# The last eight odd tiles of a dilated convolution: transposes and projections over two overlapping blocks of 128 columns, so that all TensorE operations there have one shape

## The chip, the cores and the metric

The kernel runs on one core of one Trainium2 chip. Times are device microseconds of one execution. Every run quoted here was of the state "fast"; nothing is concluded from a slow one. TensorE (PE, its weight loads PEld), VectorE (DVE), ScalarE (ACT), GpSimd (POOL) and SyncE (SP) are the engines; "SPq" lines of a profile are instructions on SyncE's own sequencer, here issues of DMA stores.

## The reference, cut to what matters

```python
B, T, D, K = (2, 16000, 144, 15)           # x: B,T,D   w: K,D,2D   w_o: D,D   all bf16
h = sum over i of xp[:, pad - 2*i : pad - 2*i + T, :] @ w[i]      # 15 taps, dilation 2
z = tanh(h[..., :D]) * sigmoid(h[..., D:])
return z @ w_o
```

The point that matters is D = 144 = 128 + 16: for the last product each tile of z must be turned round, and 144 channels do not fit in the 128 rows or columns of the array.

## The kernel before: the parts that the change and the argument touch

Each of the 128 partitions owns 250 successive positions. A *tile* is one position for all partitions: 128 x 144 values of z in the SBUF tensor `Z`. Eight tiles make an octet, kept side by side in a slot of `Z` (8 x 144 = 9 x 128 columns). All octets but the last two are turned round by a DMA transpose of nine whole blocks of 128 columns and projected with `WOR`, which holds `w_o` at every row offset that such a block can need, with zeros elsewhere.

The last two octets are handled differently so that the end of the kernel does not wait for that DMA. Their even tiles still take it; their odd tiles (dl = 1, 7, 3, 5, in two octets: eight tiles, four pairs) are transposed on TensorE, evicted from PSUM, projected, evicted again and stored pair by pair. This is that part:

```python
def ship_pair(o0, o1, dl):
    zs = (zslot(o0, dl), zslot(o1, dl))          # the two octets' slots
    pa, pb = _Bank(), _Bank()                    # two PSUM banks
    ...
    for i in range(2):
        fns.append(transpose(PSb[:, bank pa, 128*i : ...],    Z[:, zs[i], dl*D : dl*D + 128]))      # 128*128
        fns.append(transpose(PSb[0:16, bank pb, 128*i : ...], Z[:, zs[i], dl*D + 128 : dl*D + D]))  # 128*16
    g.add("dve", ... tensor_copy(zt(q, 0, 256), bank pa) ...)               # Xr<-PS on VectorE
    g.add("act", ... activation(zt(q, 256, 256)[0:16], bank pb, Copy) ...)  # Xr<-PS on ScalarE
    for i in range(2):
        fns.append(matmul(PS[:, ...], lhsT=zt(q, 128*i, 128),                rhs=WOR[:, 0, :]))     # 128*128
        fns.append(matmul(PS[:, ...], lhsT=zt(q, 256 + 128*i, 128)[0:16, :], rhs=WOR[0:16, 1, :]))  # 16*128
    g.add("act", ... activation(OS, PS, Copy) ...)                          # OS<-PS on ScalarE
...
for dl in dls[:2]:  ship_pair(o0, o1, dl)
for dl in dls[:2]:  store_both(o0, o1, dl)       # one store of 72 KB for the pair
for o in (o0, o1):
    project_some(o, (0, 2, 4, 6)); store_some(o, 0)
for dl in dls[2:]:  ship_pair(o0, o1, dl); store_both(o0, o1, dl)
...
def _(e):                                        # SyncE's program
    emit("sp", e)                                # all loads, DMA transposes and stores, in order
    for s, v in g.finals: e.wait_ge(s, v)        # then every DMA semaphore once
```

A list scheduler in the kernel puts the operations of each engine in order from estimated durations. (Here and in the diffs below access patterns are shortened.)

## Time and profile before

The median is 333.14 us (332.87 to 333.17 in three runs); the profiled run spans 331.2 us.

| What | before |
|---|---|
| PE busy, share of the span | 98% |
| first of these transposes starts | 320.05 us |
| first product of the last gate unit (line 727) starts | 322.06 us |
| end of ScalarE's last eviction | 328.11 us |
| SyncE begins to issue the last store | 328.61 us |
| span ends | 331.2 us |

From the page of before, section 1 (busy time, share of the span, instructions):

```profile
PE 323.0 (98%) x2736; PEld 249.4 (75%) x2736; DVE 302.6 (91%) x662; ACT 259.4 (78%) x626; POOL 17.2 (5%) x30
```

TensorE bounds the kernel, but a busy PE says nothing of how fast its instructions follow one another. For that, take the chain of waits of before in the tail: start, length of the step, engine, destination and line. L772 and L773 are the transposes of 128 and of 16 columns, L863 an ordinary projection, L780 and L782 the pair's projections over 128 and over 16 rows.

```profile
320.21 0.06 PE PS L772
320.27 0.15 PE PS L773
320.42 0.16 PE PS L772
320.58 0.15 PE PS L773
320.74 0.61 PE PS L863 x8
...
323.57 0.06 PE PS L780
323.64 0.16 PE PS L782
323.80 0.17 PE PS L780
...
327.48 0.20 PE PS L782
327.67 0.02 issue
327.70 0.41 ACT OS L786
```

An operation that follows one of the same shape takes a step of 0.06 us; after every change of shape the step is 0.15 to 0.17 us. The weight loads show where the time goes: here the first load of 16 columns begins 0.15 us after the start of the transpose ahead of it (320.20 against 320.05 us). The timeline of before (start, length, engine, line, operation) shows what this does to the rest. The last gate unit's input from VectorE was ready at 320.25 + 0.77 = 321.02 us, yet its first product starts at 322.06, behind two pairs of transposes and the ordinary projections between them (a gate unit is here the group of products that one tanh and one sigmoid read):

```profile
320.25 0.77 DVE L1024 TENSOR_TENSOR PS<-PS,Xp 128x576 f32<-128x576 f32 x1
322.06 0.41 PE L727 MATMUL PS<-WA,GD 128*128 128x288 bf16 x2
324.61 1.42 SPq L808 DMA_DIRECT2D out_dram<-OS  x2
327.04 0.35 SPq L851 DMA_DIRECT2D out_dram<-OS  x1
327.43 0.42 SPq L799 DMA_DIRECT2D out_dram<-OS  x1
327.70 0.41 ACT L786 ACTIVATE OS<-PS 128x288 bf16<-128x288 f32 x1 [0.28 <-PE PS L782]
327.90 1.32 SPq L808 DMA_DIRECT2D out_dram<-OS  x2
```

The last lines are the end: ScalarE evicts the last pair (the bracket says that it idled 0.28 us for TensorE), and SyncE issues the remaining stores. The last line is two issues of 0.61 us each; the second begins at 328.61 us.

### The profile page before, as it was taken

What the parts mean: (1) busy time and instruction counts of PE and PEld (TensorE: products, weight loads), DVE (VectorE), ACT (ScalarE), POOL (GpSimd) and SP (SyncE); (2) the same over time, 40 slices, a digit from 0 to 9 for tenths busy, and PEclk for the clock granted to TensorE, in tenths of its full rate; (3) what the DMA queues carried; (4) which work ended last, traced back from release to release, by engine and by line L of the source; (5) the groups of instructions that cost most, each with busy time, mean ns of one, the idle gap of its engine ahead of it and who ended that gap; (6) DMA issues with size and microseconds to landing.
All of it is one profiled execution on the core that took longest, in us unless ns stands there. A gap on an engine that the chain in (4) does not pass through costs nothing.

```text
span 331.2 us, 7123 instructions
## 1 busy us (share of the span) xinstructions
PE 323.0 (98%) x2736; PEld 249.4 (75%) x2736; DVE 302.6 (91%) x662; ACT 259.4 (78%) x626; POOL 17.2 (5%) x30
## 2 busy tenths in 40 slices
PE   7899999999999999999999999999999999999995
PEld 7787867777777777777777777777777777777773
DVE  1999889999999999999999999999999999895682
ACT  3327577979798897979798897979889797787754
POOL 8740000000000000000000000000000000000000
PEclk9999999999999999999999999999999999999997
DMA  8889942928759392956839394874919194411443
GB/s 213 265 124 210 218 121 43 191 84 169 174 99 206 81 207 100 182 158 126 218 63 194 117 177 135 146 200 93 248 38 200 38 154 117 97 48 38 107 109 107
DMA packets 112509, 46.46 MB, mean 140 GB/s; under 512 B 103822, under 2 KB 106303, under 8 KB 112477
## 3 DMA queue, kind: packets, MB, share of 16 engines
q1 hardware_dynamic: 111961, 45.68, 64.6%
q8 instruction: 21, 0.34, 0.4%
q0 software_dynamic: 512, 0.33, 0.4%
q14 instruction: 11, 0.09, 0.1%
q10 hardware_dynamic: 4, 0.01, 0.0%
HBM read 11.82 MB, written 9.22 MB: 64 GB/s over the span
## 4 chain that ended last, share of the span: by engine, by line
PE 93%; DVE 5%; ACT 1%; issue 1%; POOL 0%; POOLq 0%
PE PS L727 81%; PE PS L832 8%; DVE Xp L1012 2%; PE PS L541 1%; DVE WC L616 1%; DVE V L673 1%; DVE PS L1033 0%; PE PS L782 0%; PE PS L863 0%; PE PS L780 0%; PE PS L773 0%; DVE XA L574 0%; PE PS L772 0%; DVE PS L1024 0%; DVE Z L756 0%
## 5 line engine op out<-in xcount | busy, mean ns | idle before, releaser
L1012 DVE TENSOR_TENSOR Xp<-PS,UX 128x576 f32<-128x576 f32 x90 | 65.2, 752 | 7.0 <-PE PS L727 6.4
L1024 DVE TENSOR_TENSOR PS<-PS,Xp 128x576 f32<-128x576 f32 x90 | 68.2, 758 | 3.6 <-ACT UX L960 1.8
L727 PE MATMUL PS<-WA,GD 128*128 128x288 bf16 x360 | 69.8, 286 | 0.3 <-DVE PS L1024 0.3
L748 ACT ACTIVATE TS<-PS 128x288 f16<-128x288 f32 x125 | 51.4, 411 | 14.7 <-PE PS L727 10.0
L891 ACT ACTIVATE PS<-PS 128x288 f32<-128x288 f32 x120 | 45.4, 401 | 17.5 <-PE PS L727 17.5
L751 ACT ACTIVATE TS<-PS 128x288 f16<-128x288 f32 x125 | 50.7, 405 | 0.0
L960 ACT ACTIVATE UX<-PS 128x576 f32<-128x576 f32 x60 | 39.0, 651 | 14.7 <-PE PS L727 13.4
L727 PE MATMUL PS<-WS,GU 128*128 128x288 bf16 x210 | 44.1, 286 | 0.0
L655 ACT ACTIVATE STB<-XBc 128x512 bf16<-128x512 bf16 x60 | 35.9, 630 | 10.0 <-DVE V L673 5.6
L840 ACT ACTIVATE OS<-PS 128x432 bf16<-128x432 f32 (+1 forms) x88 | 42.4, 488 | 0.5
L832 PE MATMUL PS<-WOR,ZT 128*128 128x144 bf16 (+1 forms) x322 | 42.3, 253 | 0.0
L727 PEld LDWEIGHTS PS<-WA,GD 128*128 128x128 bf16 x360 | 34.2, 98 | 10.4 <-DVE PS L1024 0.8
L756 DVE TENSOR_TENSOR Z<-TS 128x288 bf16<-128x288 f16 x125 | 37.3, 300 | 4.0 <-ACT TS L751 3.8
L727 PE MATMUL PS<-WB,XB 128*128 128x288 bf16 x140 | 37.6, 286 | 0.0
L727 PE MATMUL PS<-WB,BF 128*128 128x288 bf16 x120 | 34.3, 286 | 0.0
L727 PE MATMUL PS<-WB,BE 128*128 128x288 bf16 x120 | 34.3, 286 | 0.0
L832 PEld LDWEIGHTS PS<-WOR,ZT 128*128 128x128 bf16 x322 | 28.0, 98 | 6.1 <-ACT OS L840 0.6
L727 PE MATMUL PS<-WD,DD 128*128 128x288 bf16 x180 | 31.9, 286 | 0.2 <-ACT PS L891 0.2
L727 PE MATMUL PS<-WA,DD 128*128 128x288 bf16 x180 | 30.9, 287 | 0.3
L727 PE MATMUL PS<-WC,V 128*128 128x288 bf16 x180 | 30.6, 286 | 0.0
L727 PE MATMUL PS<-WT,DU 128*128 128x288 bf16 x120 | 24.8, 288 | 0.7 <-DVE Xp L1012 0.7
L727 PEld LDWEIGHTS PS<-WS,GU 128*128 128x128 bf16 x210 | 20.2, 98 | 5.7 <-ACT PS L891 0.3
(89 smaller groups left out, 521.2 us busy)
## 6 DMA issues: line engine op xcount, KB each, us to landing
Xr<-in_x_dram SPq DMA_DIRECT2D x15, 576.0 KB, 4.0
out_dram<-OS SPq DMA_DIRECT2D x29, 288.0 KB, 2.8
WA<-in_w_dram SPq DMA_DIRECT2D x3, 288.0 KB, 5.0
ZT<-Z SPq DMA_TRANSPOSE x32, 3.4
Xp<-in_x_dram SPq DMA_DIRECT2D x2, 252.0 KB, 5.3
XA<-STA SPq DMA_TRANSPOSE x30, 3.2
XB<-STB SPq DMA_TRANSPOSE x30, 3.7
Xp<-in_x_dram SPq DMA_DIRECT2D x1, 441.0 KB, 4.0
```

The lines of the kernel that those rows point to most:

```text
L541: g.add("pe", [lambda t: t.matmul(PS[:, BANK_O * 512:BANK_O * 512 + 128], lhsT=ID[:], rhs=ONES[:], start=True, stop=True)] * n, r=["ID", " ...
L655: return v.activation(STB[:, q, 4 * h:4 * h + 4, :], src, ACT.Copy)
L727: return lambda t: t.matmul(bank(bk.b), lhsT=lhs(), rhs=rhs(), start=start, stop=True, skip_group_check=True)
L748: return a.activation(TS[:, s, 0, :, :], both(bk, 0, D), ACT.Tanh)
L751: return a.activation(TS[:, s, 1, :, :], both(bk, D, D), ACT.Sigmoid)
L756: return v.tensor_tensor(dst, TS[:, s, 0, :, :], TS[:, s, 1, :, :], ALU.mult)
L832: return t.matmul(PS[:, c0:c0 + n * D], lhsT=ZT[:, zt, blk, :], rhs=WOR[:, wi:wi + n, :].rearrange("p a b -> p (a b)"), start=first, stop= ...
L840: return e.tensor_copy(dst, src) if eng == "dve" else e.activation(dst, src, ACT.Copy)
L891: g.add("act", lambda e: e.activation(bank(bk.b + 1), bank(bk.b), ACT.Copy), w=[bk], dur=t_act(N2), prio=0)
L960: g.add("act", lambda e: e.activation(UX[:, k, u % NU, :, :], both(X, 0, N2), ACT.Copy), r=[X], w=[("UX", k, u % NU)], frees=[X], dur=t_ac ...
L1012: g.add("dve", lambda v, k=k, wi=wi, vb=vb, us=us: v.tensor_tensor(wslot(wi), both(vb, 0, N2), UX[:, k, us, :, :], ALU.add), r=[vb, ("UX", ...
L1024: return v.tensor_tensor(both(d, 0, N2), src, wslot(wi), ALU.add)
```

## The change

The intent is to have no small operation left. For a tile the two blocks of 128 columns are now the 128 that end with the tile (16 to 143 of its channels) and the 128 that end with its first 16 channels (112 columns of the neighbouring tile and channels 0 to 15). They cover the tile without a remainder. Of the second block 112 rows are foreign, and they meet zero rows: `WOR[:, 14]` has rows 0 to 15 of `w_o` in its last 16 rows and zeros above, `WOR[:, 15]` has rows 16 to 143.

```diff
+    LASTU = "Y0a O2 O1 Y0b D11 D00 D10 Y01 D01 O0"
...
-            for i in range(2):
-                fns.append(transpose(PSb[:, bank pa, ...],    Z[:, zs[i], dl * D:dl * D + 128]))
-                fns.append(transpose(PSb[0:DB, bank pb, ...], Z[:, zs[i], dl * D + 128:dl * D + D]))
+            for c0, bk in ((dl * D - 112, pa), (dl * D + DB, pb)):
+                for i in range(2):
+                    fns.append(transpose(PSb[:, bank bk, ...], Z[:, zs[i], c0:c0 + 128]))
-            g.add("pe", fns, r=[("Z", zs[0], dl), ("Z", zs[1], dl), "ID"], ...)
+            g.add("pe", fns, r=[("Z", z, d) for z in zs for d in (dl - 1, dl)] + ["ID"], ...)
-            ... tensor_copy(zt(q, 0, 256), bank pa) ... dur=0.21
+            ... tensor_copy(zt(q, 0, 256), bank pa) ... dur=0.33
-            ... activation(zt(q, 256, 256)[0:DB, :], PSb[0:DB, bank pb], ACT.Copy)
+            ... activation(zt(q, 256, 256), PSb[:, bank pb], ACT.Copy)
-            lhsT=zt(q, 128 * i, 128), rhs=WOR[:, 0, :]
-            lhsT=zt(q, 256 + 128 * i, 128)[0:DB, :], rhs=WOR[0:DB, 1, :]
+            lhsT=zt(q, 256 * k + 128 * i, 128), rhs=WOR[:, 14 + k, :]          # k in (0, 1)
...
-            for name, off in pattern:
+            for name, off in (pattern if t < NUN - 1 else last_pattern):
```

`LASTU`, the order of the last unit's items, is what the old pattern gives there anyway.

More of the change, by code (lines that the diff above doesn't have):

```diff
@@ L770, in ship_pair @@
             fns = []
-            for i in range(2):
-                fns.append(lambda t, i=i: t.transpose(PSb[:, pa.b * 1024 + 128 * i:pa.b * 1024 + 128 * i + 128], Z[:, zs[i], dl * D:dl * D + 128], ID[:]))
-                fns.append(lambda t, i=i: t.transpose(PSb[0:DB, pb.b * 1024 + 128 * i:pb.b * 1024 + 128 * i + 128], Z[:, zs[i], dl * D + 128:dl * D + D], ID[:]))
-            g.add("pe", fns, r=[("Z", zs[0], dl), ("Z", zs[1], dl), "ID"], alloc=[pa, pb], dur=0.24, floating=True)
-            g.add("dve", lambda v: v.tensor_copy(zt(q, 0, 256), PSb[:, pa.b * 1024:pa.b * 1024 + 256]), r=[pa], w=[("ZTL", q, 0), ("Xr", 0)], frees=[pa], dur=0.21, prio=0)
-            g.add("act", lambda a: a.activation(zt(q, 256, 256)[0:DB, :], PSb[0:DB, pb.b * 1024:pb.b * 1024 + 256], ACT.Copy), r=[pb], w=[("ZTL", q, 1)], frees=[pb], dur=0.29, prio=0)
+            for c0, bk in ((dl * D - 112, pa), (dl * D + DB, pb)):
+                for i in range(2):
+                    fns.append(lambda t, i=i, c0=c0, bk=bk: t.transpose(PSb[:, bk.b * 1024 + 128 * i:bk.b * 1024 + 128 * i + 128], Z[:, zs[i], c0:c0 + 128], ID[:]))
+            g.add("pe", fns, r=[("Z", z, d) for z in zs for d in (dl - 1, dl)] + ["ID"], alloc=[pa, pb], dur=0.24, floating=True)
+            g.add("dve", lambda v: v.tensor_copy(zt(q, 0, 256), PSb[:, pa.b * 1024:pa.b * 1024 + 256]), r=[pa], w=[("ZTL", q, 0), ("Xr", 0)], frees=[pa], dur=0.33, prio=0)
+            g.add("act", lambda a: a.activation(zt(q, 256, 256), PSb[:, pb.b * 1024:pb.b * 1024 + 256], ACT.Copy), r=[pb], w=[("ZTL", q, 1)], frees=[pb], dur=0.29, prio=0)
             bo = _Bank()
@@ L779, in ship_pair @@
             for i in range(2):
-                fns.append(lambda t, i=i: t.matmul(PS[:, bo.b * 512 + i * D:bo.b * 512 + i * D + D], lhsT=zt(q, 128 * i, 128), rhs=WOR[:, 0, :],
-                                                   start=(i == 0), stop=True, skip_group_check=True))
-                fns.append(lambda t, i=i: t.matmul(PS[:, bo.b * 512 + i * D:bo.b * 512 + i * D + D], lhsT=zt(q, 256 + 128 * i, 128)[0:DB, :], rhs=WOR[0:DB, 1, :],
-                                                   start=False, stop=True, skip_group_check=True))
+                for k in range(2):
+                    fns.append(lambda t, i=i, k=k: t.matmul(PS[:, bo.b * 512 + i * D:bo.b * 512 + i * D + D], lhsT=zt(q, 256 * k + 128 * i, 128), rhs=WOR[:, 14 + k, :],
+                                                            start=(i == 0 and k == 0), stop=True, skip_group_check=True))
             g.add("pe", fns, r=[("ZTL", q, 0), ("ZTL", q, 1)] + wor_keys, alloc=[bo], dur=0.26, floating=True)
@@ L1181, in _conv_wavenet_kernel @@
         pattern = [(x.rstrip("+"), x.count("+")) for x in PATTERN.split()]
+        last_pattern = [(x, 0) for x in LASTU.split()]
         reach = max(o for _, o in pattern)
@@ L1230, in _conv_wavenet_kernel @@
         m, r, o0, o1 = octs(NUN - 1)
-        dorder = [x for x, _ in pattern if x[0] == "D"]
+        dorder = [x for x, _ in last_pattern if x[0] == "D"]
         dls = [{"D00": 7, "D01": 5, "D10": 3, "D11": 1}[x] for x in dorder]
```

## The prediction

> What bounds it now. TensorE: the page has PE busy 98%, and the chain of waits gives PE 93%. The change touches only the last 8 us. There the chain of waits is unbroken TensorE work from 317.3 to 327.7 us, then one 0.41 us ScalarE eviction; after it SyncE issues the last stores, and the span ends at 331.2 us.
>
> In that tail the timeline shows what is slow. Projections that keep the 128x128 shape step by 61 ns (eight of L863 in 0.49 us of weight loads). The pair code alternates 128x128 with 128x16 (transposes) and with 16x128 (projections): the chain shows steps of 0.15 to 0.16 us for those transposes and 0.16 to 0.17 us for those projections. 16 transposes and 16 projections at about 0.16 us take 5.1 us. The Trainium skill, "TensorEngine Tiling (Array Packing)", Key Properties, says that changing the tiling mode drains the TensorE. The steps agree: about 0.1 us for every change of shape.
>
> What the change does.
> - Removes about 31 changes of shape. The same 32 operations at 61 ns take 2.0 us: about 3.1 us less on TensorE.
> - Adds none: instruction counts stay. ScalarE's copy becomes 128x256 in place of 16x256; its 0.37 us goes by the free size and should stay. VectorE's copy stays at 0.29 us. The new reads of the neighbouring tile are of data written a pair earlier: no new wait.
> - Moves nothing else: the order given for the last unit equals the old one once the look-ahead items are dropped. The scheduler's 0.21 to 0.33 us for VectorE's copy may swap a few tail operations, or make it pick another pass: the main uncertainty.
>
> What of it is critical. The first two pairs stand in TensorE's order before the last gate unit: its first product (322.06 us) waited behind them, while its VectorE input was ready at 321.02 us. Without the drains it starts near 321.2, 0.85 us earlier. After it, TensorE has 0.62 us of ordinary projections, four pairs of blocks and 4 L863: 2.2 us in place of 4.4.
>
> But ScalarE then has no gaps left: from about 322.15 us (the unit's tanh) it must do 0.82 (tanh, sigmoid) + 0.54 + 0.38 (L840) + 2 x 0.37 (L776) + 4 x 0.41 (L786) = 4.1 us, so it ends near 326.2, not 328.1. The last SyncE stores (0.35 + 0.42 + 2 x 0.61 us) follow as closely as now; landing stays 2.2 us. So of 3.1 us about 1.9 come out; the rest turns into TensorE waiting for ScalarE's evictions.
>
> Predicted: 331.2 us (333.1 - 1.9), eight times in ten 330.3 to 332.4. Faster by over 2%: 0.01; within 2%: 0.98; slower by over 2%: 0.01.
>
> What would show each step right or wrong.
> - Timeline: transposes and pair projections step by about 61 ns.
> - The first product of the last gate unit starts near 321.2 us.
> - The chain at the end runs through ScalarE (L776, L786, L840) or SyncE's stores instead of TensorE; PE is idle between 323 and 326 us, with ScalarE as releaser.
> - The copy L776 stays at 0.37 us with 128 partitions.
> - Nothing changes before 319 us.
>
> What would make it wrong.
> - The step comes from the alternating banks, not the shape: then it stays, and the gain is under 1 us.
> - The schedule changes upstream, or the tail's evictions come in another order: half a microsecond either way.
> - SyncE's issue, not ScalarE, sets the end: gain 1.5 us.

## The result, and the profile after

After: 331.82 us (331.25 to 332.2, six runs), before beside it 333.15 us (332.66 to 333.61, six runs). The ratio is 0.9958, with a 95% interval of 0.9944 to 0.9973: about 1.4 us faster. In two later groups of runs the same after-to-before comparison gave 0.9952 (the kernel after unchanged) and 0.9955 (a variant that proved identical in time, below).

Section 1 of the page after:

```profile
PE 320.5 (97%) x2736; PEld 248.8 (75%) x2736; DVE 302.6 (92%) x662; ACT 258.7 (78%) x626; POOL 17.9 (5%) x30
```

The chain of waits of after, in the tail (L774 are the transposes, L782 the pair's projections, L777 ScalarE's copy of the transposed block, L786 and L840 evictions of projections):

```profile
320.75 0.22 PE PS L774 x4
320.97 0.50 PE PS L863 x8
321.47 0.23 PE PS L774 x4
321.70 0.30 PE PS L863 x4
322.01 0.73 PE PS L728 x6
322.74 0.63 PE PS L832 x7
...
323.91 0.61 ACT OS L786 x2
324.52 0.57 ACT Xr L777 x2
325.09 0.30 ACT OS L840
325.39 0.70 ACT OS L786 x2
```

Four transposes take 0.22 us, one step of 0.06 us each, and from 323.4 us on the chain runs through ScalarE, no longer through TensorE. The timeline of after:

```profile
320.78 0.77 DVE L1024 TENSOR_TENSOR PS<-PS,Xp 128x576 f32<-128x576 f32 x1
321.84 0.41 PE L728 MATMUL PS<-WA,GD 128*128 128x288 bf16 x2
322.78 0.41 ACT L749 ACTIVATE TS<-PS 128x288 f16<-128x288 f32 x1 [0.66 <-PE PS L728]
323.08 0.41 ACT L752 ACTIVATE TS<-PS 128x288 f16<-128x288 f32 x1
324.24 1.42 SPq L808 DMA_DIRECT2D out_dram<-OS  x2
325.31 0.78 ACT L786 ACTIVATE OS<-PS 128x288 bf16<-128x288 f32 x2
325.70 0.61 SPq L851 DMA_DIRECT2D out_dram<-OS  x1
326.36 0.42 SPq L799 DMA_DIRECT2D out_dram<-OS  x1
326.83 1.32 SPq L808 DMA_DIRECT2D out_dram<-OS  x2
```

The two spans must not simply be subtracted. The profiled run of after came 0.5 us later to the tail, for a reason that has nothing to do with the change. Timeline of before, then of after, at the first large block of products:

```profile
14.85 11.19 PE L727 MATMUL PS<-WA,XA 128*128 128x288 bf16 x90
```

```profile
15.25 11.19 PE L728 MATMUL PS<-WA,XA 128*128 128x288 bf16 x90
```

The same instructions start 0.40 us later there. Over the profiled runs that start varies from 13.96 to 15.25 us, and the stretch from there to the first transpose from 305.2 to 305.9 us. So everything below is measured from the start of the first transpose of the tail, in each run's own timeline (a store has landed when the trace shows the last update of its completion semaphore):

| From the first transpose to | before | after | earlier by |
|---|---|---|---|
| last gate unit's first product | 2.01 us | 1.26 us | 0.75 us |
| end of ScalarE's last eviction | 8.06 us | 5.51 us | 2.55 us |
| SyncE begins the last store's issue | 8.56 us | 6.96 us | 1.60 us |
| last store has landed | 10.68 us | 9.09 us | 1.59 us |
| end of the span | 11.17 us | 9.57 us | 1.60 us |

(To two digits the spans are 331.22 and 330.15 us.) The computing is over 2.55 us sooner, and about a microsecond of it is given back between the last eviction and the last store's issue. That gap was 0.50 us and is now 1.45 us. In the timeline of after, SyncE's six issues stand back to back from 324.24 us to 328.15 us; in before they had a pause of a microsecond.

### The profile page after: what moved, and what is told of

It reads as the page before. It is cut to its first block, busy times and chain, and to the rows that moved or that the text cites. A ratio compares the mean times of both kernels' runs of the same rounds, so it can differ in the third digit from the quotient of the medians.

```text
span 330.2 us, 7124 instructions
## 1 busy us (share of the span) xinstructions
PE 320.5 (97%) x2736; PEld 248.8 (75%) x2736; DVE 302.6 (92%) x662; ACT 258.7 (78%) x626; POOL 17.9 (5%) x30
## 4 chain that ended last, share of the span: by engine, by line
PE 92%; DVE 4%; ACT 2%; issue 1%; POOL 0%; POOLq 0%
PE PS L728 81%; PE PS L832 8%; DVE Xp L1012 2%; PE PS L542 1%; DVE WC L617 1%; DVE V L674 1%; DVE PS L1033 0%; PE PS L566 0%; ACT OS L786 0%; ACT XA L575 0%; ACT OS L840 0%; PE PS L863 0%; DVE PS L1024 0%; DVE Z L757 0%; ACT UX L960 0%
## 5 line engine op out<-in xcount | busy, mean ns | idle before, releaser
L840 ACT ACTIVATE OS<-PS 128x432 bf16<-128x432 f32 (+1 forms) x88 | 42.4, 488 | 0.5
```

The costliest lines, as they stand in the source:

```text
L840: return e.tensor_copy(dst, src) if eng == "dve" else e.activation(dst, src, ACT.Copy)
```

## The experiments

Twelve runs were made, of eleven new kernels and of the kernel after once more; all gave correct results. The distances are from the profile of each run, as in the table above; times have five rounds (five or six runs), ratios are to before in the same rounds.

| Run | last eviction | last issue on SyncE | last landing | end | median us | ratio to before |
|---|---|---|---|---|---|---|
| before | 8.06 | 8.56 | 10.68 | 11.17 | 333.15 | 1 |
| after | 5.51 | 6.96 | 9.09 | 9.57 | 331.82 | 0.9958 |
| after_again | 5.51 | 6.98 | 9.11 | 9.59 | 331.64 | 0.9952 |
| e1_alternate_banks | 5.51 | 6.97 | 9.10 | 9.59 | 331.81 | 0.9955 |
| e2_group_shapes | 6.50 | 7.33 | 9.45 | 9.94 | 331.89 | 0.9963 |
| e3_projections_only | 6.77 | 7.75 | 9.88 | 10.36 | 332.26 | 0.9970 |
| e4_transposes_only | 6.61 | 7.07 | 9.19 | 9.68 | 331.62 | 0.9957 |
| e5_last_store_act | 5.50 | 6.26 | 8.99 | 9.74 | 332.29 | 0.9972 |
| e6_double_evictions | 6.24 | 6.99 | 9.11 | 9.60 | 331.56 | 0.9947 |
| e7_three_queues | 5.51 | 5.78 | 8.82 | 9.57 | 331.75 | 0.9955 |
| e8_pool_store | 5.50 | 6.43 | 8.80 | 9.49 | 331.80 | 0.9953 |
| e9_final_waits | 5.51 | 6.97 | 9.09 | 9.59 | 331.37 | 0.9945 |
| e10_relief_after | 5.51 | 6.10 | 8.59 | 9.08 | 331.19 | 0.9934 |
| e11_relief_before | 8.30 | 8.33 | 10.50 | 10.99 | 333.22 | 0.9998 |

The intervals of these ratios are about 0.0012 to 0.0018 to either side (0.4 to 0.6 us), so a few tenths of a microsecond are read from the timelines, not from the times. The row of e11 needs care: its profiled run lost TensorE clock before the last eviction (below).

### Is it the shape? Four runs

The theory is the prediction's: each change of shape costs TensorE about 0.1 us. One rival was named there: the old code also alternated between two PSUM banks, and the change happens to group by bank.

**e1_alternate_banks** is the kernel after with the old order of banks.

```diff
-            for c0, bk in ((dl * D - 112, pa), (dl * D + DB, pb)):
-                for i in range(2):
+            for i in range(2):
+                for c0, bk in ((dl * D - 112, pa), (dl * D + DB, pb)):
```

> The kernel after, with its four transposes of a pair in the old order of banks (first bank, second, first, second); all shapes stay 128x128. From the first of these transposes to the end of the last ScalarE eviction the kernel before takes 8.06 us (320.05 to 328.11) and after 5.51 us (320.58 to 326.09); to the end of the span 11.15 and 9.62 us. Theory (the cost is the change of shape): transposes step by 0.06 us, 5.5 and 9.6 us again, time within 0.3 us of after. Rival (the cost is the alternation of two PSUM banks): transposes step by 0.15 us, the transposes' half of the gain is lost, about 6.8 us to the last eviction.

Measured: the chain has the four transposes in 0.22 and 0.23 us as before the edit, and all distances are those of after. The banks play no part.

**e2_group_shapes** is the kernel before, small shapes and all, but with like beside like: two changes of shape for a group of four in place of four.

```diff
             for i in range(2):
                 fns.append(transpose(bank pa, Z[..., dl * D:dl * D + 128]))      # 128*128
+            for i in range(2):
                 fns.append(transpose(bank pb, Z[..., dl * D + 128:dl * D + D]))  # 128*16
```

(and the same line between the projections over 128 and over 16 rows).

> The kernel before, with the same small shapes, but the two 128x128 operations of each group of four ahead of its two small ones: 2 changes of shape for a group in place of 4. Theory (a change of shape costs about 0.1 us): a group of four takes 0.43 us in place of 0.62, steps inside a shape are 0.06 us, about 1.5 us less TensorE time in 8 groups, about 6.6 us to the last eviction. Rival (a small operation is slow in itself, as its weights load slower): groups stay at 0.62 us, 8.1 us to the last eviction, time of before.

The chain of e2 (L772 and L774 the two kinds of transposes, L781 and L784 the two kinds of projections):

```profile
320.15 0.11 PE PS L772 x2
320.26 0.21 PE PS L774 x2
320.47 0.61 PE PS L865 x8
...
323.23 0.23 PE PS L784 x2
323.46 0.23 PE PS L781 x2
```

Two small transposes take 0.21 us, one step of 0.15 and one of 0.06. The eight ordinary products that follow take 0.61 us against 0.50 in after, where no change precedes them. So a group costs two times 0.10 us for its two changes, 0.32 + 0.11 = 0.43 us as expected, and a small operation behind one of its own shape is as quick as a large one. The rival, a slow small operation, is refuted. The last eviction comes at 6.50 us (expected 6.6).

**e3_projections_only** and **e4_transposes_only** each do half of the change. In e3 the second projection takes all 128 rows; those beyond 16 hold old finite data and meet zero rows of `WOR[:, 1]`. In e4 the second transpose takes 128 columns, 112 of them foreign and never used (`Z` got 112 columns more at its end for this, `Zf`).

```diff
# e3
-   lhsT=zt(q, 256 + 128 * i, 128)[0:DB, :], rhs=WOR[0:DB, 1, :]
+   lhsT=zt(q, 256 + 128 * i, 128),          rhs=WOR[:, 1, :]
# e4
-   transpose(PSb[0:DB, bank pb, ...], Z[:, zs[i], dl * D + 128:dl * D + D])
+   transpose(PSb[:, bank pb, ...], Zf[:, (zs[i] * 8 + dl) * D + 128:(zs[i] * 8 + dl) * D + 256])
```

> The kernel before, with only the projections' second weight load and product taken over all 128 rows (the other rows of the weight matrix are zero); transposes stay 128x16. Theory: projections step by 0.06, transposes by 0.15 us; the last gate unit's first product still starts about 2.0 us after the first transpose (before: 2.01), the last eviction ends about 6.5 us after it. Both parts should carry about half of the 2.55 us. Rival (only the transposes drain): 8.0 us.

> The kernel before, with only the second transpose of each tile taken over 128 columns (16 of its own and 112 of whatever follows), the projections as before on 16 rows. Theory: transposes step by 0.06, projections by 0.165 us; the last gate unit starts about 1.2 us after the first transpose (after: 1.26), the last eviction ends about 6.7 us after it. Rival (only the 16-row projections drain): 8.0 us and the gate unit at 2.0 us.

Each removed the steps of 0.15 to 0.17 us of its own half and left the other's. The gate unit starts at 2.01 us in e3 and 1.22 us in e4: it is the transposes alone that stand in its way. At the last eviction e3 gains 1.29 us and e4 1.45 us of the 2.55, so the halves about add up. At the last store's issue they do not: e4 alone gains 1.49 us there and the whole change 1.60. With the transposes already done, the second half of the computing gain is worth only 0.11 us at the last issue. This is the first sign that something other than TensorE and ScalarE has taken over.

### What took a microsecond back? Eight runs

The prediction's account was that after the change ScalarE's evictions set the end and the stores follow them as closely as before. The rival, named in the prediction as a way for it to fail, is that SyncE's issuing of stores sets the end. **after_again** is the kernel after, the reference for the three runs beside it.

> The kernel after, unchanged, as the reference for the three runs beside it: 331.8 us (331.25 to 332.2), 9.6 us from the first transpose to the end of the span.

It came as expected: 9.6 us, 331.64 us.

**e6_double_evictions** makes ScalarE later on purpose: an idle eviction of the same size, to dead memory, ahead of each of its last two.

```diff
+            idle = [activation(Xr[:, 1, ...], PS[:, bank bo, 0:2 * D], ACT.Copy)] if dl in (3, 5) else []
-            g.add("act", activation(OS, PS[:, bank bo, 0:2 * D], ACT.Copy), ...)
+            g.add("act", idle + [activation(OS, PS[:, bank bo, 0:2 * D], ACT.Copy)], ...)
```

> The kernel after, with an idle eviction of the same size (0.41 us) ahead of each of ScalarE's last two, which puts its last one about 0.75 us later, 6.25 us after the first transpose. Theory (SyncE's issue ends the tail): the last store is issued at 6.96 us all the same, the span ends at 9.6 us, the time is that of after_again. Rival, the one of the prediction (ScalarE's evictions set the end and the stores follow): 10.3 us, 0.75 us slower.

The timeline of e6:

```profile
325.35 0.41 ACT L786 ACTIVATE Xr<-PS 128x288 bf16<-128x288 f32 x1
325.61 0.42 SPq L800 DMA_DIRECT2D out_dram<-OS  x1
325.65 0.40 ACT L787 ACTIVATE OS<-PS 128x288 bf16<-128x288 f32 x1
326.08 1.33 SPq L809 DMA_DIRECT2D out_dram<-OS  x2
```

The last eviction ends 0.73 us later (6.24 against 5.51 us), the last store is issued at 6.99 us as if nothing had happened, and the time is 331.56 us, not slower than after_again at 331.64. This is the decisive run: after the change ScalarE has 0.7 us to spare, and the prediction's account of the end is wrong.

**e5_last_store_act** and **e7_three_queues** take stores away from SyncE: in e5 the last one goes to ScalarE's queue, in e7 one more to GpSimd's.

```diff
# e5 and e7
-            store_both(o0, o1, dl)
+            store_both(o0, o1, dl, "sp" if dl != dls[3] else "act")
# e7
-            store_some(o, 0)
+            store_some(o, 0, "sp" if o == o0 else "pool")
```

> The kernel after, with its last store issued from ScalarE's queue, which is free once its last eviction is done (5.51 us after the first transpose), in place of SyncE's, where it is issued 6.96 us after (327.54 us) behind five others that stand back to back. Theory (in the kernel after, SyncE's issue of stores ends the tail): SyncE's last issue is then the one of 6.25 us, ScalarE's comes near 5.6 us, the span ends 0.7 us earlier, 8.9 us after the first transpose, and the time falls by about 0.7 us against after_again. Rival (ScalarE's evictions or the landing end the tail): no gain, 9.6 us.

> As e5_last_store_act, and the second store of even tiles is issued from GpSimd's queue, which is idle. Theory: SyncE has four stores left after its first, the last issued about 5.8 us after the first transpose; ScalarE's is issued near 5.6 us; the span ends near 8.4 us, 1.1 to 1.2 us earlier than after_again, near 330.7 us. What may spoil it: GpSimd's stores land later (its loads took 2.6 to 4.5 us), but it is issued near 4.5 us. Rival (issue is not the limit): no gain over e5_last_store_act.

Both failed. SyncE's last issue came earlier as expected (6.26 and 5.78 us), yet the span ended at 9.7 and 9.6 us, and e5 was even 0.6 us slower than after_again in the medians (the intervals overlap; in the timelines 0.15 us). The reason is in the landings. The issue is not the end; the end is the *landing* of the last store, and after it SyncE's waits. In e5 ScalarE's store, issued at 325.96 us, landed at 329.10, 3.1 us later, where in after a store takes 2.1 to 2.5 us; SyncE's own last store took 2.7 us. The summary of waits on SyncE's sequencer of e5 shows the rest (L1269 is the loop of final waits; us in total, times, longest):

```profile
SPq L1269 <- DMA out_dram<-OS: 0.8, 1, 0.8
```

That wait stands in the middle of the list, with ten more waiting instructions of about 0.06 us behind it. So the span ended 0.75 us after the last landing, in after 0.48 us. In e7 the wait for GpSimd's store, second in the list, held the others up by 1.2 us, and the last of them ran after the last landing. A store handed to another queue was paid for in landing time, its own and that of others, and in the order of the waits. The theory in its first form, "the issue ends the tail", was too coarse.

**e8_pool_store** does less: a single store, one with time in hand, goes to GpSimd's queue.

```diff
-            store_some(o, 0)
+            store_some(o, 0, "sp" if o == o0 else "pool")
```

> The kernel after, with one of the six last stores (even tiles of the second octet, 0.42 us of SyncE's issue) issued from GpSimd's idle queue at about 4.2 us after the first transpose; it lands in 3.1 us there, well ahead of the end. What the three runs before this showed: in every run with all stores on SyncE the span ends 2.6 to 2.7 us after SyncE's last store issue begins (before 328.61 to 331.2, after 327.54 to 330.2), whatever ScalarE does; e5 failed because a store issued from ScalarE's queue took 3.1 us to land in place of 2.2 and 22 other final waits stood behind its wait. Theory: SyncE's last issue begins 0.47 us earlier, at 6.5 us after the first transpose, the span ends at 9.15 us, 0.45 us earlier than after. Rival (the end has another cause, e5 and e7 showed it): 9.6 us.

SyncE's last issue moved by the expected 0.5 us (6.43 us), the last landing by 0.29 us (8.80 us), the span's end by 0.1 us (9.5 us). The last two stores now took 2.7 and 2.4 us to land in place of 2.3 and 2.1, and the GpSimd store's final wait, early in the list, held the others up by 0.4 us. Only a part of the expected gain came.

**e9_final_waits** settles whether those final waits matter in the kernel after: they are cut to the stores' six semaphores (the loads have been waited for by their users).

```diff
-        self.finals = [(slot[0], slot[1]) for p in pools.values() for slot in p]
+        self.finals = [(slot[0], slot[1]) for tag in ("sq", "st") for slot in pools.get(tag, [])]
```

> The kernel after, with SyncE's waits after its last store cut from 50 semaphores (25 instructions, 329.3 to 330.8 us in before, 1.5 us) to the 6 of the stores (the loads were waited for by their users). Theory A (the landing of the last store, 2.2 us after its issue begins, ends the span; the 25 instructions run beside it): 9.5 to 9.6 us after the first transpose as in after. Theory B (those instructions end the span): 8.5 us, over 1 us faster. From the numbers the two nearly tie in after (0.61 + 1.5 against 2.2 us), so I expect a gain of at most 0.1 us.

Its summary of SyncE's waits has a line that after does not have:

```profile
SPq L1269 <- DMA out_dram<-OS: 1.4, 3, 0.7
```

SyncE now really waits for landings, and the end is where it was: last landing 9.09 us, span 9.6 us. So the landing of the last store ends the kernel after, and the 25 waiting instructions run beside it (in after they take from 328.20 to 329.71 us, and the last landing is at 329.67: nearly a tie).

**e10_relief_after** and **e11_relief_before** put the pieces together. Two stores that come early go to GpSimd's queue, and the final waits are cut as in e9. The same edit is made to the kernel after and to the kernel before.

```diff
-            store_some(o, 0)
+            store_some(o, 0, "sp" if o == o0 else "pool")
-            store_both(o0, o1, dl)                                    # dl in dls[:2]
+            store_both(o0, o1, dl, "pool" if dl == dls[0] else "sp")
         # and the edit of e9
```

> The kernel after, with two of the last six stores (first odd tile, even tiles of the second octet) issued from GpSimd's queue, and only the stores' semaphores waited for at the end. Theory: SyncE's last issue begins as soon as the data and one issue ahead of it allow, 6.1 to 6.2 us after the first transpose in place of 6.96; the span ends near 8.8 us, 0.8 us earlier than after, about 331.0 us: faster than both kernels. Rival: 9.6 us.

> The kernel before with the same relief of SyncE as e10_relief_after. Theory (the change's gain is held up at SyncE): before gains less, about 0.45 us (its last data come at 8.06 us, its last issue moves from 8.56 to 8.1 us), 10.7 us to the end of the span. The change alone, with the stores relieved in both, is then worth 1.9 us (10.7 against 8.8) in place of 1.5 (11.15 against 9.6). Rival (SyncE plays no part): both gain the same and the difference stays 1.5.

The timeline of e10, SyncE's issues of stores:

```profile
324.06 0.76 SPq L808 DMA_DIRECT2D out_dram<-OS  x1
324.93 0.54 SPq L851 DMA_DIRECT2D out_dram<-OS  x1
325.51 1.48 SPq L808 DMA_DIRECT2D out_dram<-OS  x2
```

In e10 SyncE's last issue comes at 6.10 us (after: 6.96) and the last landing at 8.59 us (after: 9.09). Its median is 331.19 us, ratio 0.9934 (0.9922 to 0.9946): the fastest kernel, 2.2 us (333.3 x 0.0066) faster than before. Against after it is faster by 0.5 us in the timeline; the two intervals of the ratios still touch. In e11 the same relief gives the kernel before nothing in the times (0.9998, 0.9985 to 1.0011) and 0.2 us in the timeline: its last eviction is at 8.30 us, its last issue at 8.33. But that timeline is not a clean one. In the profiled run of e11 the granted TensorE clock falls from 1.00 to 0.50 at 326.25 us, with four projections still to come. In before it falls at 327.49 us, when the last one has already begun; in after and e10 only after TensorE's last product. The chain of waits of e11 there:

```profile
326.22 0.17 PE PS L782
326.39 0.23 PE PS L780
326.63 0.23 PE PS L782
```

Four steps of 0.23 in place of 0.17 us are what puts the last eviction at 8.30 and not at 8.06 us. With relief in both, the change of shapes is worth 10.99 - 9.08 = 1.9 us in the timelines, but about 1.7 us once those 0.24 us of clock are taken off (an estimate from these steps), against 1.6 us without relief. In the times of the same rounds it is 333.0 - 331.1 = 1.9 us (means), with intervals of 0.4 us to either side of each ratio. That does not tell the expected 1.9 us from the 1.5 us of the rival, so it is not shown that the relief is worth more to the kernel after than to the kernel before. Why the clock falls there, and how often it does so in runs that were not profiled, no run here shows.

What e10 does show is that in the kernel after an earlier issue brings an earlier end. Even so not all arrives: against after, the last issue comes 0.86 us earlier, the last landing 0.50 us, the end 0.49 us. The last landing follows the last issue's start by 2.13 us in after, by 2.17 in e11 and by 2.49 in e10. The Trainium skill, "DMA: Bandwidth & Descriptors", Anatomy of one DMA, gives a DMA on GpSimd's path about 2.0 us of fixed time plus its bytes over 436 GB/s, by which e10's two stores from GpSimd should take 2.2 us (72 KB) and 2.3 us (144 KB; both are estimates from that page). They took 2.14 and 3.25 us, so it fits the first and not the second; the stores that land last are SyncE's. The same page, Issuing engines are not separate DMA queues, says that issuing from several engines saves only the sequencer's time. This agrees: e10 saved 0.86 us of issue, and 0.5 us of it reached the end. Why a landing takes 2.1 us in one run and 2.5 or more in another stays open. By the view of busy times by window the DMA engines were busy for 80% of the stretch from 325.0 to 328.3 us of e10, but also for 76% of that from 325.7 to 329.2 us of after. Stores that delay one another would fit; no run took transfers away to show it.

## Why the prediction was right or wrong

The time was inside the range, and the forecast of 1.9 us is to be held against 1.4 us measured (0.9 to 1.9 by the interval) and 1.6 us in the timelines.

- *The cost of a change of shape, 0.1 us, and 3.1 us of TensorE time in all.* Right. The steps fell to 0.06 us; e1 excluded the banks, e2 showed the cost at each change and not at the small operation, e3 and e4 split it into halves. The Trainium skill, "TensorEngine Tiling (Array Packing)", Key Properties, names a mechanism: a change of tiling mode drains the TensorE. It gives no size; here it is 0.09 to 0.11 us. The runs show the price of a change and that the next weight load comes later; no run tells a drain from a load that is merely not taken ahead.
- *The gate unit starts 0.85 us earlier.* It started 0.75 us earlier.
- *Nothing else moves; the copy with 128 partitions keeps its 0.37 us.* Right: the same order on all engines, and 0.38 to 0.39 us for the copy.
- *ScalarE then has no gaps and needs 4.1 us from the tanh on, so 1.9 us come out.* Right in kind, wrong in size: ScalarE works from 322.78 to 326.09 us without a pause, but in 3.31 us. The sum added whole durations. In the timeline of after, tanh starts at 322.78 us and the sigmoid at 323.08, 0.30 us later, though each lasts 0.41 us. The Trainium skill, "ScalarE: Activation LUTs", What ACT_TABLE_LOAD costs, says that back-to-back activations overlap by about 93 ns; here it is 0.11 us. The timeline of before already has that overlap (tanh at 322.99, sigmoid at 323.30 us, 0.41 us each), so it could have been read off before predicting. So 2.55 us came out at the last eviction, not 1.9.
- *"The last SyncE stores (0.35 + 0.42 + 2 x 0.61 us) follow as closely as now".* This is the step that failed. The gap from the last eviction to the last issue grew from 0.50 to 1.45 us. The sum counted four issues behind the last L840 and left out the two ahead of them, which now leave SyncE no pause; the L851 issue took 0.61 us in place of 0.35. Of the 0.95 us that the gap grew, 0.27 us is L851 waiting behind those two (it starts 0.30 us after the L840 that it needs, before 0.03), 0.27 us the longer way from its start to the last issue (1.84 against 1.57 us), and 0.41 us ScalarE itself, which now ends 0.69 us after that L840 in place of 1.10, while the stores do not come faster. e6 shows that ScalarE could be 0.7 us later for nothing. "SyncE's issue, not ScalarE, sets the end: gain 1.5 us" stood in the prediction among what would make it wrong, and this is what happened, with the amendment from e5, e8 and e9 that the end proper is the landing of the store issued last.

The two wrong terms have opposite signs, +0.65 and -0.95 us. That they nearly cancel is why the total was close; a total that fits does not prove its terms.

## What to carry to other kernels

If a small remainder (16 of 144 here) alternates with full blocks on TensorE, overlap the blocks and zero the weights rather than cut a small one, or at least put like shapes side by side, which here brought 1.56 of 2.55 us at the last eviction for an edit of two lines; in the time of the whole kernel e2, e4 and after cannot be told apart (0.9963, 0.9957, 0.9958). When a tail gets shorter, add up the whole queue of stores behind it, issue times first and then the landing of the last one, before counting the gain: six issues of 0.4 to 0.75 us were hidden behind slower computing and came to light. Compare traces from an event near the change, since half a microsecond of unrelated start-up difference was as large as the effects sought.

## What the Trainium skill lacked or had wrong

- "TensorEngine Tiling (Array Packing)", Key Properties: it says that a change of mode drains the TensorE, but not what that costs. Here each change adds 0.09 to 0.11 us to a step of 0.06 us, for 128 to 16 columns and for 128 to 16 rows alike.
- "TensorE: Matmul & The Clock Gate", LDWEIGHTS: it gives the load's time as the number of columns over 1.2 GHz, so 13 ns for 16 columns. The records of the trace last 85 ns for loads of 16 columns and 96 ns for those of 128; how much of a record is a fixed part the runs do not tell. Loads of one shape overlap and follow each other every 0.06 us.
- The same page, Back-to-back issue gap: about 81 ns for each pair of weight load and product of 128 columns in a sustained stream. Here four such transposes take 0.22 us (56 ns each) and eight products of 144 columns 0.50 us (62 ns each). The formula that the section keeps for a single product, columns over 2.4 GHz plus 2.5 ns, fits both (55.8 and 62.5 ns).
- "DMA: Bandwidth & Descriptors": it has no figure for this chip by name for how long a store's issue holds SyncE; the nearest is 512 sequencer cycles for each plain DMA instruction of "previous generations", in a table about another chip. In the kernel after an issue takes 0.33 to 0.75 us for stores of 72 to 288 KB, not in the order of their size, and this is what held up the tail. A store from ScalarE's queue landed after 3.1 us and one from SyncE's, issued 0.7 us later in the same run, after 2.7 us, against 2.1 to 2.5 us in the kernel after.
- None of the pages I read has the cost of the final waits: two semaphores for each waiting instruction, one instruction every 0.06 us, 1.5 us for 50 semaphores. It is hidden behind the landing only as long as no slow landing stands early in the list.
